# Routing kernel: where the sums of W1's quarters are made, and how the first token group is multiplied

## The chip, the cores and the metric

The kernel runs on one core of a Trainium2 chip. The core has a matrix engine (PE, with its weight loads PEld), a vector engine (DVE), an activation engine (ACT), a general engine (POOL) and a queue engine for transfers (SP), and DMA queues. The metric is the device time of one execution in microseconds. One profiled execution gives a trace, in which times count from the first instruction.

## The reference: attention, routing, experts

The input is q, k, v of 8 batches x 8 heads x 576 positions x 64. First comes a causal attention with a window of 128 and a distance bias per head. Its result is laid out as x, 4608 tokens x 512. Then

```
logits = x @ w_gate ; P = exp(logits - max)            # 4608 x 8
eight times: rows of P to sum 1, columns of P to sum N/E
out = sum over e of P[:, e] * ( relu(x @ w1[e]) @ w2[e] )    # w1: 512 x 1024, w2: 1024 x 512
```

so every token goes through all eight experts, and the expert outputs are weighted by P. As P is not negative, scaling x by P[:, e] ahead of the first layer gives the same result as scaling the output; the kernel uses that for experts 2 to 7.

## The kernel before: stages, queues and order

The schedule is written by hand: every engine takes its instructions in the order in which the program issues them.

**Up to P.** The attention runs block by block. Into it a `Filler` weaves experts 0 and 1, which are multiplied with unscaled x and whose outputs are stored in DRAM (`ysp`) until P is known. The filler deals out pieces: a first-layer piece `l1` (four matmuls of 512 columns, counted as 0.87 us, followed by a ReLU on ACT, L127) or a second-layer piece `l2` (eight matmuls, 1.74 us, followed by a cast on DVE, L555, and later a store on SP, L541). `filler.fill(us)` issues pieces until the given time less 0.3 is reached. Then eight rounds of normalisation of P run on DVE (L825 to L852), with pieces woven in.

**Experts 2 to 7.** From line 861 on, the 36 blocks of 128 tokens are taken as 18 groups of two blocks. A unit is one group with one expert, so there are 18 x 6 = 108 units. A unit computes the first layer of its own expert and, woven in, the second-layer products of the unit before (`product(n - 1, ...)`). The second layer always takes seven products of quarter matrices (a Strassen scheme): the sums of W2's quarters are made once per expert by `sums_of`, five DVE operations of 128x1024 each (L630), and those of the activations by `make_sums` in each unit (L991 to L993).

The first layer has two forms:
- **plain** (`l1_bank`, L953): 32 matmuls of 256 columns in four PSUM banks, each followed by a ReLU on ACT;
- **in seven products** (`part`, L974): 56 matmuls of 128 columns. It needs the sums of W1's quarters from `quads_w1` (four DVE operations of 128x1024, L934; the last one overwrites quarter a21, so the plain form can't be used for that expert behind it), and the sums of x's quarters T1 to T4 from `sums_x` (three DVE operations, L910 to L912). Three PSUM banks A, B and C are filled and copied into each other: A is copied to B (L1126), C to `s5` (L1130), B to C (L1135). L1141 on DVE adds bank B and `s5`, and only then part a22 may go into bank B; L1145 does the same for bank C.

Before the change the first group (units 0 to 5) takes the plain form and all others the other one. `quads_w1` for an expert is called in the unit behind that expert's plain unit.

**Transfers of x.** `scale_x(n)` on ACT multiplies a unit's x with P, two operations (L888); `turn_xs(n)` on SP transposes it with two DMAs (L898). In a unit n both are done for unit n + 2. SP also carries the stores of expert 0 and 1, the loads of their outputs (`load_y`) and the output itself (`finish`).

**Gathering.** A group's seven products add up in the PSUM banks `Ms` over its six experts. The first unit of the next group finishes the last expert's products; `gather` on DVE then adds the banks into `acc` (L1055): products 3, 4, 5 and 2 in that unit, 6, 7 and 1 in the one behind it (`done`). `finish` sends `acc` out.

**The list of sums.** `todo` holds DVE operations that are issued a few at a time by `some(n)`: W2's sums of experts 2 to 4 behind the last attention steps and in the rounds of P, seven more at L857, the rest in units 0 to 4:

```
some((4, 1, 0, 3, 2)[n] if n < 5 else 0)
if 0 < n <= E - 2:
    quads_w1(units[n - 1][1])
```

Of the kernel before, what the change touches and what calls it, by code (L numbers as in the profile page):

```python
# [14 lines left out]
def kernel(  # L15
# [213 lines left out]
    if True:  # L229
# [387 lines left out]
        def extras(e):  # L617
            for n in range(3 if e == E - 3 else e - 1):
                if n not in more:
                    at = dict(tag="a8", bufs=8) if n < 2 else {}  # L620
                    t = (per if n < 2 else lp).tile([P, 4, NF2, HB], FP16, name=f"more_{n}", **at)
                    more[n] = [t[:, i] for i in range(4)]
            return more[e - 2][0:3] if e < E - 3 else [more[n][3] for n in range(3)]

        def sums_of(e, f1, f3, f4):
            q = W2L[e]
            q.update(f1=f1, f3=f3, f4=f4, f6=q["q12"], f7=q["q21"])

            def one(to, x, y, op):
                nc.vector.tensor_tensor(out=q[to], in0=q[x], in1=q[y], op=op)  # L630

            return [
                lambda a=a: one(*a)
                for a in (
                    ("f1", "q11", "q22", ALU.add),
                    ("f3", "q12", "q22", ALU.subtract),
                    ("f4", "q11", "q21", ALU.subtract),
                    ("f6", "q11", "q12", ALU.add),
                    ("f7", "q21", "q22", ALU.add),
                )  # L640
            ]

        def some(n):
            for _ in range(min(n, len(todo))):
                todo.pop(0)()
# [207 lines left out]
        store()  # L853
        filler.fill(1.6)

        todo += sums_of(5, *extras(5))
        some(7)  # L857

# [12 lines left out]
        xs = [xset[i // 2][:, 4 + 2 * (i % 2) : 6 + 2 * (i % 2), :].rearrange("p q n -> p (q n)") for i in range(4)]  # L873

        def strassen(n):
            return n >= E - 2

        def load_x(g):
            for m in range(2):
# [14 lines left out]
        def turn_xs(n):  # L894
            if n >= N:
                return
            for m in range(2):
                nc.sync.dma_start(  # L898
                    out=xset[n % 2][:, 2 * m : 2 * m + 2, :].rearrange("p q (d t) -> p (q d) t", t=P),
                    in_=xs[2 * (n % 2) + m],  # L900
                    transpose=True,
                )
# [11 lines left out]
        def quads_w1(e):  # L914
            w = W1L[e]
            q = dict(a11=w[:, 0:2, 0:HF], a12=w[:, 2:4, 0:HF], a21=w[:, 0:2, HF:Fd], a22=w[:, 2:4, HF:Fd])
            if e < E - 2:
                t = lp.tile([P, 3, 2, HF], FP16, name=f"s_{e}")
                q.update(s1=t[:, 0], s2=t[:, 1], s3=t[:, 2])
            elif e == E - 1:  # L920
                t = per.tile([P, 2, 2, HF], FP16, name=f"s_{e}", tag="xT", bufs=4)
                q.update(s1=t[:, 0], s2=t[:, 1])
                q["s3"] = [per.tile([P, HF], FP16, name=f"s3_{k}", tag="yo", bufs=YO) for k in range(2)]
            else:
                q.update((f"s{i}", aux[:, i].rearrange("p f n -> p (f n)").rearrange("p (k f) -> p k f", k=2)) for i in (1, 2, 3))
            q["s4"] = q["a21"]
            SL[e] = q

            def one(to, a, b, op):
                if isinstance(q[to], list):  # L930
                    for k in range(2):
                        nc.vector.tensor_tensor(out=q[to][k], in0=q[a][:, k], in1=q[b][:, k], op=op)
                else:
                    nc.vector.tensor_tensor(out=q[to], in0=q[a], in1=q[b], op=op)  # L934

            one("s1", "a21", "a22", ALU.add)
            one("s3", "a11", "a21", ALU.subtract)
            one("s2", "s1", "a11", ALU.subtract)
            one("s4", "a12", "s2", ALU.subtract)

        def new_h(n):
            h[n] = per.tile([P, 8, NF2, P], FP16, name=f"hs_{n}", tag="hT", bufs=2)
# [93 lines left out]
        def gather(g, *which):  # L1036
            q4 = acc.rearrange("p m (c n) -> p (m c) n", c=2)
            for m in which:
                bk, half = BANK[m]
                ps = Ms[bk][:, half, :]  # L1040
                for lo, step, op in {
                    1: ((0, 3, ALU.add),),
                    2: ((2, 0, ALU.add), (3, 0, ALU.subtract)),
                    3: ((1, 2, ALU.add),),
                    4: ((0, 2, ALU.subtract),),
                    5: ((0, 0, ALU.subtract), (1, 0, ALU.add)),
                    6: ((3, 0, ALU.add),),
                    7: ((0, 0, ALU.subtract),),
                }[m]:
                    if step:  # L1050
                        a = q4[:, lo : lo + step + 1 : step, :]
                        p2 = ps.unsqueeze(1).to_broadcast([P, 2, HB])
                    else:
                        a, p2 = q4[:, lo, :], ps
                    nc.vector.tensor_tensor(out=a, in0=a, in1=p2, op=op)  # L1055
# [32 lines left out]
        scale_x(0)  # L1088
        scale_x(1)
        turn_xs(0)  # L1090
        filler.fill(3.0)
        while filler.fill(5.0):
            pass
        store()
        load_last(E - 1)
        w2f = per.tile([P, 4, NF2, HB], FP16, name="w2f", tag="w1t", bufs=2)
        todo += sums_of(6, F1_6, w2f[:, 2], w2f[:, 3]) + sums_of(7, aux[:, 0], w2f[:, 0], w2f[:, 1])
        s5y = per.tile([P, 2, GT], FP32, name="s5y", tag="xTt", bufs=1)
        s5 = s5y[:, 0].rearrange("p (f t) -> p f t", f=NF2)
        y = s5y[:, 1].bitcast(FP16).rearrange("p (m d) -> p m d", m=2)  # L1100
        turn_xs(1)
        xs[:] = [per.tile([P, HD], FP16, name=f"xs_{i}", tag="yo", bufs=YO) for i in range(2)] * 2
        late: tuple = ()
        for n in range(N):
            g = units[n - 1][0]
            end = ends(n - 1)
            done, late = late, ()
            if n > 0:
                make_sums(n - 1)
            some((4, 1, 0, 3, 2)[n] if n < 5 else 0)  # L1110
            if 0 < n <= E - 2:
                quads_w1(units[n - 1][1])
            if done:
                gather(units[n - 2][0], 6, 7)
                gather(units[n - 2][0], 1)
            if n > 0 and units[n - 1][1] == 6:
                begin(g, 1)
            y_first_half = n > 0 and units[n - 1][1] == (5 if g == groups[0] else 4)
            if y_first_half:
                begin(g, 0)  # L1120
            if strassen(n):
                new_h(n)
                pa = bank(n, "A")
                part(n, pa, "a11", B11, True)
                pb = bank(n, "B")
                nc.scalar.copy(out=pb, in_=pa)  # L1126
                product(n - 1, 3)
                pc = bank(n, "C")
                part(n, pc, "s1", T1, True)
                nc.scalar.copy(out=s5, in_=pc)  # L1130
                product(n - 1, 4)
                if end:
                    gather(g, 3, 4)
                part(n, pb, "s2", T2)
                nc.scalar.copy(out=pc, in_=pb)  # L1135
                part(n, pa, "a12", B21)
                relu(n, 0, pa)
                scale_x(n + 2)
                product(n - 1, 5, 2)
                part(n, pb, "s3", T3)  # L1140
                nc.vector.tensor_tensor(out=h[n][:, 3], in0=pb, in1=s5, op=ALU.add)  # L1141
                relu(n, 3, h[n][:, 3])
                part(n, pc, "s4", B22)
                turn_xs(n + 2)
                nc.vector.tensor_tensor(out=h[n][:, 1], in0=pc, in1=s5, op=ALU.add)  # L1145
                relu(n, 1, h[n][:, 1])
                sums_x(n + 1)
                if end:
                    gather(g, 5, 2)
                product(n - 1, 6, 7)  # L1150
                part(n, pb, "a22", T4)
                relu(n, 2, pb)
                product(n - 1, 1)
            else:
                pairs = ((3, 4), (5, 2), (6, 7), (1,))
                for i in range(4):
                    l1_bank(n, i)
                    if i == 1:
                        scale_x(n + 2)
                    product(n - 1, *pairs[i])  # L1160
                    if end and i in (0, 1):
                        gather(g, *pairs[i])
                turn_xs(n + 2)
                sums_x(n + 1)
            if done:
                finish(units[n - 2][0])
            if n > 0 and units[n - 1][1] == 2:
                load_y(g, 0)
            if y_first_half:
                load_y(g, 1)  # L1170
            if end:
                late = (6, 7, 1)
            if n == N - E + 2:
                load_w2(E - 1)
# [34 lines left out]
```

## Time and profile before

| what | us |
| --- | --- |
| three runs: median (lowest to highest) | 1025.03 (1024.62 to 1025.8) |
| the profiled execution | 1025.63 |
| its span from first to last instruction | 1023.9 |
| PE busy | 1000.3 |
| DVE busy | 749.5 |
| ACT busy | 722.2 |
| last rounds of P end on DVE | 326.3 |
| expert 1's last pieces end on PE, unit 0 begins | 342.6 |
| unit 6 (the first in seven products) begins | 380.5 |
| unit 107, the last, begins | 1010.1 |

The rounds of P take the stretch up to 326 us, then come the last pieces of experts 0 and 1 up to 342.6, then the units; the change touches the time from 326 us on. A line of the timeline gives start and duration in us, engine, line, operation, output and inputs with their shapes, how many equal ones were merged, and in brackets the idle time of the engine before it with the one who ended it. The end of a matmul is modelled and overlaps the next one's start; the starts are what to go by.

### The profile page before, as it was taken

Reading aid. Unit: us, or ns where it says so; the run is one execution under the profiler, and the core shown is the slowest. Engines: PE = TensorE matmul, PEld = TensorE weight load, DVE = VectorE, ACT = ScalarE, POOL = GpSimd, SP = SyncE. Lnnn points to the kernel's source line nnn. Section 1 sums busy time; section 2 is a strip of 40 time slices with the busy share of each in tenths; the row PEclk is TensorE's granted clock in tenths of the full one; section 3 lists DMA queues with packets and bytes.
Section 4 is the critical chain, followed back from the end, with each engine's and each line's share of the span. In section 5 each row is a group of like instructions: output and inputs, shape, how many; then the busy total and the mean of one; then the engine's idle time right before and its main releaser. Section 6 shows DMA issues by size and latency. Waiting matters only on the chain.

```text
span 1023.9 us, 27787 instructions
## 1 busy us (share of the span) xinstructions
PE 1000.3 (98%) x11487; PEld 801.6 (78%) x11487; DVE 749.5 (73%) x1594; ACT 722.2 (71%) x1240; POOL 78.8 (8%) x143
## 2 busy tenths in 40 slices
PE   7999999999999999999999999999999999999998
PEld 5645444444544698999999999999999999999997
DVE  5735665556578588877877877877887887787787
ACT  7646555555433457888888888888888888888885
POOL 1212033306110000000000000000000000000000
PEclk9999999999999999999999999999999999999999
DMA  9996689889999233343334334324334434333461
GB/s 244 219 271 170 143 221 220 191 196 180 221 192 177 69 72 80 71 81 94 74 64 100 76 66 94 73 64 94 77 65 98 81 71 81 86 82 65 98 115 47
DMA packets 264431, 122.46 MB, mean 120 GB/s; under 512 B 201968, under 2 KB 255728, under 8 KB 264304
## 3 DMA queue, kind: packets, MB, share of 16 engines
q1 hardware_dynamic: 249568, 102.68, 44.2%
q0 software_dynamic: 14304, 17.84, 10.5%
q8 instruction: 90, 1.47, 0.6%
q14 instruction: 37, 0.30, 0.1%
q10 hardware_dynamic: 432, 0.16, 0.1%
HBM read 78.30 MB, written 23.59 MB: 100 GB/s over the span
## 4 chain that ended last, share of the span: by engine, by line
PE 74%; DVE 3%; DMA 1%; ACT 1%; issue 0%; DVEq 0%; ACTq 0%; SPq 0%
PE psM L1011 30%; PE psB L974 13%; PE psA L974 9%; PE psC L974 9%; PE psy L137 5%; PE psh L115 5%; PE psh L953 2%; DVE acc L1055 1%; PE psN L468 1%; DMA acc<-xd 0%; DVE hs L1141 0%; PE psS L412 0%; DVE hs L991 0%; DVE hs L992 0%; DMA s5y<-ysp 0%
## 5 line engine op out<-in xcount | busy, mean ns | idle before, releaser
L1011 PEld LDWEIGHTS <-hs 128*128 128x128 f16 x2996 | 271.7, 98 | 22.4
L1011 PE MATMUL psM<-w2l,hs 128*128 128x256 f16 x1440 | 186.6, 273 | 0.0
L974 PEld LDWEIGHTS <-w1l 128*128 128x128 f16 x2720 | 173.2, 98 | 8.9 <-issue 3.0
L127 ACT ACTIVATE hT<-psh 128x512 f16<-128x512 f32 (+1 forms) x144 | 83.3, 586 | 100.9 <-PE psh L115 100.2
L987 ACT ACTIVATE hs<-hs 128x512 f16<-128x512 f16 x204 | 125.0, 630 | 34.3 <-DVE hs L1141 34.1
L1141 DVE TENSOR_TENSOR hs<-psB,s5y 128x512 f16<-128x512 f32 x102 | 70.4, 690 | 103.7 <-ACT xs L888 95.9
L115 PE MATMUL psh<-xT,w1t 128*128 128x512 f16 (+1 forms) x608 | 139.8, 368 | 3.2 <-DVE xT L517 2.4
L974 PEld LDWEIGHTS <-s 128*128 128x128 f16 x2040 | 135.3, 98 | 5.8
L888 ACT ACTIVATE xs<-xtok,L_sb 128x512 f16<-128x512 f16 x204 | 136.0, 720 | 0.6 <-DMA xset<-xs 0.6
L137 PE MATMUL psy<-w2t,hT 128*128 128x512 f16 x576 | 134.3, 379 | 0.0
L1011 PE MATMUL psM<-more,hs 128*128 128x256 f16 x864 | 129.0, 273 | 0.0
L974 PE MATMUL psA<-xset,w1l 128*128 128x128 f16 x1360 | 103.7, 219 | 0.0
L974 PE MATMUL psB<-xset,s 128*128 128x128 f16 x1360 | 103.7, 219 | 0.0
L137 PEld LDWEIGHTS <-hT 128*128 128x128 f16 x576 | 53.5, 98 | 60.9 <-issue 1.5
L555 DVE CAST yo<-psy 128x512 f16<-128x512 f32 x68 | 46.8, 690 | 72.1 <-PE psy L137 57.8
L115 PEld LDWEIGHTS <-w1t 128*128 128x128 f16 x608 | 54.7, 98 | 54.7 <-issue 7.0
L991 DVE TENSOR_TENSOR hs<-hs 128x1024 f16<-128x1024 f16 x107 | 74.0, 691 | 23.5 <-ACT hs L987 16.8
L430 ACT ACTIVATE pt<-psS 128x1024 f16<-128x1024 f32 (+2 forms) x80 | 67.7, 851 | 29.2 <-PE psS L412 22.7
L1135 ACT COPY psC<-psB 128x512 f32<-128x512 f32 x102 | 58.1, 570 | 36.5 <-PE psB L974 36.5
L1130 ACT COPY s5y<-psC 128x512 f32<-128x512 f32 x102 | 59.8, 586 | 25.5 <-PE psC L974 25.5
L443 DVE TENSOR_TENSOR pt<-pt,mask 128x1024 f16<-128x1024 f16 (+2 forms) x80 | 51.8, 647 | 32.8 <-ACT pt L430 32.7
L1055 DVE TENSOR_TENSOR acc<-acc,psM 128x256 f32<-128x256 f32 (+1 forms) x162 | 74.1, 503 | 2.1
(121 smaller groups left out, 1410.1 us busy)
## 6 DMA issues: line engine op xcount, KB each, us to landing
s5y<-ysp SPq DMA_DIRECT2D x36, 256.0 KB, 3.0
ysp<-yo SPq DMA_DIRECT2D x68, 128.0 KB, 3.3
v<-in_v_dram SPq DMA_DIRECT2D x32, 256.0 KB, 4.4
out_dram<-acc SPq DMA_DIRECT2D x31, 256.0 KB, 2.5
q<-in_q_dram SPq DMA_DIRECT2D x5, 1024.0 KB, 7.8
k<-in_k_dram SPq DMA_DIRECT2D x5, 1024.0 KB, 10.1
xtok<-xd SPq DMA_DIRECT2D x34, 128.0 KB, 2.3
w2t<-in_moe_w_dram POOLq DMA_DIRECT2D x4, 1024.0 KB, 10.9
```

What stands on the lines that cost most here:

```text
L115: nc.tensor.matmul(out=ps[:, 0:nt], lhsT=w1ts[e][:, dt, P * ft : P * ft + P], rhs=xT[:, at : at + nb, dt, :], start=(dt == 0), stop=(dt == ...
L127: nc.scalar.activation(out=st["hT"][:, ft, 0:nt], in_=ps[:, 0:nt], func=AF.Relu)
L137: nc.tensor.matmul(out=ps, lhsT=st["hT"][:, ft, P * ms : P * ms + P], rhs=w2ts[e][:, ft, :], start=(ft == 0), stop=(ft == NFT - 1),)
L430: nc.scalar.activation(out=pt[0:nk, :, 0 : nk + nn], in_=ps[0:nk, :, :, 0 : nk + nn].rearrange("p a y n -> p (a y) n"), func=AF.Exp, scale ...
L888: nc.scalar.mul(out=xs[2 * (n % 2) + m], in_=xtok[m], mul=P_sb[:, blk, e : e + 1])
L974: nc.tensor.matmul(out=ps[:, j, :], lhsT=q[k][:, P * j : P * j + P], rhs=xset[n % 2][:, x, P * k : P * k + P], start=(start and j == 0 and ...
L987: nc.scalar.activation(out=h[n][:, slot], in_=src, func=AF.Relu)
L991: nc.vector.tensor_tensor(out=t[:, 4:6], in0=t[:, 0:2], in1=t[:, 2:4], op=ALU.add)
L1011: nc.tensor.matmul(out=Ms[bk][:, half, :], lhsT=h[n][:, LEFT[m], f, :], rhs=W2L[e][RIGHT[m]][:, f, :], start=(e == 2 and f == 0 and half = ...
L1055: nc.vector.tensor_tensor(out=a, in0=a, in1=p2, op=op)
L1130: nc.scalar.copy(out=s5, in_=pc)
L1141: nc.vector.tensor_tensor(out=h[n][:, 3], in0=pb, in1=s5, op=ALU.add)
```

## The change

- `sums_of(5)` and `some(7)` behind the rounds of P go. In their place the sums of W1 for experts 2, 3 and 4, then W2's sums and W1's sums of expert 5 are put on the list, and while the filler has pieces of experts 0 and 1, one sum is issued behind each piece. What is left then is issued at once (`some(len(todo))`), ahead of the last stores.
- `quads_w1` returns its four operations for the list instead of issuing them. Those of experts 6 and 7 are put on the list behind their W2 sums, and a new table says how many sums each unit issues.
- The first group's units of experts 2 to 6 take the seven-product form; only expert 7's unit stays plain. `sums_x(0)` is called ahead of the loop.
- `turn_xs(1)` is issued right behind `turn_xs(0)`, ahead of the stores of the remaining pieces.
- The gather of product 1, in the second unit of a group, moves from the head of the unit to behind L1141 and its ReLU.

```diff
@@ behind the rounds of P
-        todo += sums_of(5, *extras(5))
-        some(7)
@@ strassen(n)
-            return n >= E - 2
+            return n >= E - 2 or units[n][1] < E - 1
@@ quads_w1(e), at its end
-            one("s1", "a21", "a22", ALU.add)
-            one("s3", "a11", "a21", ALU.subtract)
-            one("s2", "s1", "a11", ALU.subtract)
-            one("s4", "a12", "s2", ALU.subtract)
+            return [
+                lambda a=a: one(*a)
+                for a in (
+                    ("s1", "a21", "a22", ALU.add),
+                    ("s3", "a11", "a21", ALU.subtract),
+                    ("s2", "s1", "a11", ALU.subtract),
+                    ("s4", "a12", "s2", ALU.subtract),
+                )
+            ]
@@ ahead of the loop over units
         turn_xs(0)
-        filler.fill(3.0)
-        while filler.fill(5.0):
-            pass
+        turn_xs(1)
+        for e in range(2, 5):
+            todo += quads_w1(e)
+        todo += sums_of(5, *extras(5)) + quads_w1(5)
+        while filler.fill(0.9):
+            some(1)
+        some(len(todo))
         store()
         load_last(E - 1)
         w2f = per.tile([P, 4, NF2, HB], FP16, name="w2f", tag="w1t", bufs=2)
-        todo += sums_of(6, F1_6, w2f[:, 2], w2f[:, 3]) + sums_of(7, aux[:, 0], w2f[:, 0], w2f[:, 1])
+        todo += sums_of(6, F1_6, w2f[:, 2], w2f[:, 3]) + quads_w1(6)
+        todo += sums_of(7, aux[:, 0], w2f[:, 0], w2f[:, 1]) + quads_w1(7)
...
-        turn_xs(1)
+        sums_x(0)
@@ in the loop over units
-            some((4, 1, 0, 3, 2)[n] if n < 5 else 0)
-            if 0 < n <= E - 2:
-                quads_w1(units[n - 1][1])
+            some({0: 5, 1: 2, 2: 2, 3: 2, 4: 2, 5: 1, 7: 1, 8: 1, 9: 1, 10: 1}.get(n, 0))
             if done:
                 gather(units[n - 2][0], 6, 7)
-                gather(units[n - 2][0], 1)
...
                 relu(n, 3, h[n][:, 3])
+                if done:
+                    gather(units[n - 2][0], 1)
                 part(n, pc, "s4", B22)
```

## The prediction

> **What bounds the kernel now.** I read the page first, then the order of work of PE and DVE around the change, then the same in a later group. The page: PE is the bound.
>
> ```profile
> PE 1000.3 (98%) x11487; PEld 801.6 (78%) x11487; DVE 749.5 (73%) x1594; ACT 722.2 (71%) x1240; POOL 78.8 (8%) x143
> ```
>
> The timeline of PE from 325 to 400 us (start, duration, what; in brackets the idle time before it and who ended it) shows the last four second-layer pieces of expert 1 (L137), then group 0.
>
> ```profile
> 335.65 7.07 PE L137 MATMUL psy<-w2t,hT 128*128 128x512 f16 x32
> 342.56 3.66 PE L953 MATMUL psh<-xset,w1l 128*128 128x256 f16 x32
> 347.79 1.03 PE L953 MATMUL psh<-xset,w1l 128*128 128x256 f16 x8 [1.57 <-DMA xset<-xset]
> ...
> 373.98 1.04 PE L953 MATMUL psh<-xset,w1t 128*128 128x256 f16 x8
> ...
> 380.53 0.61 PE L974 MATMUL psA<-xset,w1l 128*128 128x128 f16 x8
> ...
> 387.90 0.61 PE L974 MATMUL psB<-xset,w1l 128*128 128x128 f16 x8 [1.90 <-DVE hs L1141]
> ...
> 388.78 0.61 PE L974 MATMUL psA<-xset,w1l 128*128 128x128 f16 x8
> ...
> 395.40 0.61 PE L974 MATMUL psA<-xset,w1l 128*128 128x128 f16 x8
> ```
>
> Unit 0 begins at 342.56, unit 1 at 347.79, unit 5 at 373.98, units 6, 7, 8 at 380.53, 388.78 and 395.40. A plain unit with its products costs 6.55 us: (373.98 - 347.79)/4. PE loses 1.57 us to the second turned x and 1.90 us to L1141 in unit 6.
>
> The timeline of DVE over the same stretch: who could be late.
>
> ```profile
> 328.39 0.69 DVE L555 CAST yo<-psy 128x512 f16<-128x512 f32 x1 [2.10 <-PE psy L137]
> 329.00 1.28 DVE L630 TENSOR_TENSOR w2l<-w2l 128x1024 f16<-128x1024 f16 x2
> 330.20 1.89 DVE L630 TENSOR_TENSOR more<-w2l 128x1024 f16<-128x1024 f16 x3
> 332.00 1.28 DVE L630 TENSOR_TENSOR w2l<-w2l 128x1024 f16<-128x1024 f16 x2
> 333.21 0.68 DVE L555 CAST yo<-psy 128x512 f16<-128x512 f32 x1
> 337.58 0.69 DVE L555 CAST yo<-psy 128x512 f16<-128x512 f32 x1 [3.69 <-PE psy L137]
> ...
> 342.76 0.69 DVE L555 CAST yo<-psy 128x512 f16<-128x512 f32 x1 [1.03 <-PE psy L137]
> 343.37 0.68 DVE L630 TENSOR_TENSOR f<-w2l 128x1024 f16<-128x1024 f16 x1
> ...
> 350.81 0.68 DVE L934 TENSOR_TENSOR s<-s,w1l 128x1024 f16<-128x1024 f16 x1
> 351.59 0.69 DVE L934 TENSOR_TENSOR w1l<-w1l,s 128x1024 f16<-128x1024 f16 x1
> ```
>
> Two things: DVE works in written order (the seven sums of `some(7)` stand between the casts as in the code; the cast behind them begins at 333.21 although PE's piece was done at 331.64). And a sum costs 0.60 us from start to start (329.00 to 333.21 is seven), the one that reads the sum just made 0.18 more (350.81 to 351.59).
>
> A later group, DVE then PE: unit 13 begins at 426.32, 14 at 432.63, 15 at 438.82.
>
> ```profile
> 429.56 1.54 DVE L1055 TENSOR_TENSOR acc<-acc,psM 128x256 f32<-128x256 f32 x3
> 431.02 0.68 DVE L1141 TENSOR_TENSOR hs<-psB,s5y 128x512 f16<-128x512 f32 x1
> ```
>
> ```profile
> 426.32 0.61 PE L974 MATMUL psA<-xset,w1l 128*128 128x128 f16 x8
> ...
> 432.63 0.61 PE L974 MATMUL psA<-xset,w1l 128*128 128x128 f16 x8
> ...
> 438.82 0.61 PE L974 MATMUL psA<-xset,w1l 128*128 128x128 f16 x8
> ```
>
> A seven-product unit takes 6.18 us, but the second unit of a group 6.31: three gathers ahead of L1141 push it past the moment when PE needs bank B.
>
> **The change part by part.**
>
> *Sums under the last pieces.* At the loop eleven pieces are left (six first-layer, five casts: the trace has six L127 and five L555 behind the scaling of x at 329.98). The list holds 23 sums: 2 left of expert 4, 12 of W1 for experts 2 to 4, 5 of W2 and 4 of W1 for expert 5. One is issued behind each piece, twelve behind them all. Those ahead of the last cast lie in DVE's idle time (3.69 and about 1.03 before each cast) and cost nothing. The last cast stays at 342.76, since PE sets it; the eleventh sum begins at 343.37, and 13 sums, two of which read the one before, take 13 x 0.60 + 2 x 0.18 = 8.2 us: DVE is free at 351.56. There was no such queue before.
>
> *Unit 0 in seven products.* `sums_x(0)` stands behind that queue. Its first operation took 0.42 (L910), and a waiting PE starts 0.06 behind DVE's end (387.84 to 387.90), so T1 is there at 352.04. PE does part a11 at 342.56 to 343.01 and waits 9.0 us; there are no products of an earlier unit to put in. Then s1, s2, a12, s3, s4 run to about 354.7. `some(5)` stands ahead of L1141: the three x sums end at 352.55 (0.45 + 0.33 + 0.21), five W2 sums at 355.56, L1141 lasts 0.69, and part a22 into bank B starts at 356.30 and takes 0.45. Unit 1 begins at 356.75 against 347.79: +8.96, which contains the 1.57 us saved.
>
> *PE's pace behind that wait.* No wait of 9 us is in the trace; the nearest rows are the first matmuls of the run, on a PE that had done nothing yet, and the next ones of their shape.
>
> ```profile
> 1.05 4.08 PE L249 MATMUL psJ<-ones 128*128 128x256 f16 x20 [1.05 <-DVE ones L651]
> ...
> 5.77 0.60 PE L249 MATMUL psJ<-ones 128*128 128x256 f16 x4
> ```
>
> Twenty in 4.08 us is about 0.2 each, four in 0.60 (less the 0.27 of the last) is 0.11; the slow spell lasts some 3.6 us. Behind idle stretches up to 1.90 us the pace stays full. If PE falls back, s3 ends at 355.45 and L1141 waits for it: +0.14 us, the rest hides under `some(5)`. Ends: 0 (full pace) and +1.5 (slow for two such spells, to about 359.2: 2.8 us past 356.4 at half pace lose 1.4 more). I take +0.14, nearest to the row.
> The Trainium skill ("TensorE: Matmul & The Clock Gate", Part 1) says that PE falls to half clock after an idle window of about 3.4 us and returns after a busy one; windows run free, so by that rule this term would be an estimated 0.1 to 1.4 us and the sum +2.9 to +4.2, where the row alone gives +2.94. No run here has shown the fall behind a wait.
>
> *Units 1 to 4 in seven products.* 4 x (6.55 - 6.18) = 1.48 saved. Their new DVE work hides: make_sums ends some 2.5 us into a unit, two sums end at 3.7 to 3.9, and L1141 is due at 4.25 (436.88 - 432.63). In unit 4 `begin` adds 0.8 us, 0.05 late; in unit 1 ACT's copies of unit 0's end cost 0.03. I take 1.44 saved, 0 to 1.5 possible. Unit 5 stays plain, 6.55; the load of y, 0.5 us late for DVE now, comes earlier since unit 4 frees its x sooner.
>
> *W1 of expert 7 later.* The five DVE operations of 3 us ahead of unit 6's gathers go: unit 6 falls from 8.25 to 6.18, 2.06 saved. In unit 7 (6.62) one sum remains (0.60) and the last gather moves: L1141 is just in time, but `product(n-1, 1)` must wait some 0.2 us until the moved gather has read its bank. 6.40: 0.22 saved, ends 0 and 0.44. Units 8 to 10 take one more sum each in slack of over 1 us.
>
> *x turned ahead of the stores.* SP issues two transposes (2.52 us) before six stores instead of behind them; the stores end with the last cast all the same. POOL's queue is unchanged: its loads of expert 7 were issued at 307 and 318. Cost 0; the gain is counted above. If a store came late, the buffers that it frees are next written by unit 0's scaling, at about 354.
>
> *Gather of product 1 behind L1141.* In unit 13 L1141 could start at 430.57 (unit start + 4.25) once the two other gathers (0.33 each) end near 430.2. The 0.13 us goes: 15 groups x 0.13 + 0.44 in the last (a wait of that size ended at 990.62) = 2.44 saved. L1145 moves from 431.62 to 431.77, its ReLU with it, and the next copy into bank B ends at 434.1, where PE needs it at 434.27; the moved gather ends at 431.85, and bank M1 is due at 432.06. Both fit, with 0.1 to 0.2 us to spare. Ends: 0 and 2.6.
>
> **Sum:** +8.96 + 0.14 - 1.44 - 2.06 - 0.22 - 2.44 = +2.94. The profiled execution took 1025.63 us (span 1023.9 and 1.7 around it), 0.6 above the median of 1025.03. So 1028.6 by that execution, 1028.0 against the median. What a measurement of this kernel can tell from no change is 0.2%, 2.05 us, so the forecast is slower, narrowly.
>
> **Rivals.**
> 1. *The gather's gain doesn't come*, because the later L1145 or the bank of M1 holds PE up as much. For it: slacks of 0.1 to 0.2 us; against: they are positive. +5.4: 1030.4. Chance 0.13.
> 2. *PE stays slow longer*, for two spells of 3.6 us instead of one: 1.4 on top of the forecast, 1029.4. For it: the opening spell; against: one spell lies under `some(5)` almost whole, and the trace shows no second. Chance 0.12. (This is the Trainium skill's rule above at its late end.)
> 3. *A wash:* the last sums come sooner or the gains sum higher, within 2.05 us of before. It takes 1 us in my favourable terms, or two sums fewer at the end. About 1026.3. Chance 0.18.
> 4. *Faster:* the sums fit into DVE's idle time between the casts (five us of it), so that no queue stands behind the last cast. Place: 343.37. Price: 8.2 us of the sum, giving 1025.0 + 2.9 - 8.2 = 1019.8. The point where it decides: each sum less behind the cast is 0.60 us, so with 8 instead of 13 the change breaks even. Against it: one sum per piece, eleven pieces, and written order as seen. Chance 0.07.
>
> **Numbers.** The forecast has 0.50, its own range 1027.0 to 1029.2. Of the forecast and rivals 1 and 2 (0.75) about 0.04 falls inside the bound: slower 0.71; same 0.18 + 0.04 = 0.22; faster 0.07. From 1025.0 to 1031.4 leaves out rival 4, part of the wash and the sum of both slow rivals: under 0.2.
>
> **What would show it.** Right: DVE without idle from the last cast to L1141 of unit 0, some 13.5 us; a PE wait of about 9 us in bank C's part, then one of 1.5 on L1141; units 1 to 4 at 6.18; no wait in unit 6; second units of groups at 6.18. Wrong: T1 ready before 348, fewer than 12 sums behind the last cast, second units still at 6.3 or their successors longer, or matmuls of 128 columns at 0.11 us spacing past 357.

## The result and the profile after

The changed kernel took 1030.61 us (median of six, 1027.89 to 1032.39) against 1024.82 us for the kernel before in the same session (median of six, 1023.56 to 1026.72): ratio 1.0051, 95% interval 1.0033 to 1.0069 (the ratios here and below are the recorded estimates with their intervals; they aren't the quotients of the medians beside them). So it is slower, as forecast; the size forecast was +2.9 us, measured were +5.8. The profiled execution took 1030.17 us, with a span of 1028.2.

The timeline of PE in the changed kernel, around the first group (start, duration, what; in brackets the idle time before it and who ended it):

```profile
337.18 7.07 PE L137 MATMUL psy<-w2t,hT 128*128 128x512 f16 x32
344.08 0.61 PE L977 MATMUL psA<-xset,w1l 128*128 128x128 f16 x8
353.43 1.01 PE L977 MATMUL psC<-xset,s 128*128 128x128 f16 x8 [8.74 <-DVE xset L908]
354.24 1.06 PE L977 MATMUL psB<-xset,s 128*128 128x128 f16 x8
355.09 1.06 PE L977 MATMUL psA<-xset,w1l 128*128 128x128 f16 x8
356.00 1.01 PE L977 MATMUL psB<-xset,s 128*128 128x128 f16 x8
356.81 0.72 PE L977 MATMUL psC<-xset,w1l 128*128 128x128 f16 x8
357.87 0.61 PE L977 MATMUL psB<-xset,w1l 128*128 128x128 f16 x8 [0.34 <-DVE hs L1146]
358.31 0.61 PE L977 MATMUL psA<-xset,w1l 128*128 128x128 f16 x8
...
364.51 0.61 PE L977 MATMUL psA<-xset,w1l 128*128 128x128 f16 x8
...
383.06 1.04 PE L956 MATMUL psh<-xset,w1t 128*128 128x256 f16 x8
...
389.61 0.61 PE L977 MATMUL psA<-xset,w1l 128*128 128x128 f16 x8
...
395.80 0.61 PE L977 MATMUL psA<-xset,w1l 128*128 128x128 f16 x8
...
402.19 0.61 PE L977 MATMUL psA<-xset,w1l 128*128 128x128 f16 x8
```

Unit 0 starts at 344.08, does part a11 and then waits 8.74 us for T1 (L908 is the first operation of `sums_x`). Unit 1 starts at 358.31, unit 5 at 383.06, units 6, 7 and 8 at 389.61, 395.80 and 402.19. Parts s1 to s3 stand 0.8 to 0.9 us apart instead of 0.45: PE runs at half pace behind the wait. The view by windows shows the same in the granted clock (the first column behind the stretch is its length, the number ahead of the DMA share is the clock):

```profile
342.60:352.00 9.40, 2.10 (x16) 1.15 (x15) 8.93 (x15) 0.57 (x1) 0.00 (x0) 0.72 0.10 34
352.00:360.00 8.00, 6.23 (x72) 6.02 (x72) 7.55 (x16) 4.97 (x10) 0.00 (x0) 0.69 0.10 19
```

The timeline of DVE, changed kernel, from the last cast on:

```profile
344.29 0.69 DVE L555 CAST yo<-psy 128x512 f16<-128x512 f32 x1 [0.44 <-PE psy L137]
344.89 1.28 DVE L932 TENSOR_TENSOR s<-w1l 128x1024 f16<-128x1024 f16 x2
346.10 0.68 DVE L932 TENSOR_TENSOR s<-s,w1l 128x1024 f16<-128x1024 f16 x1
346.81 0.69 DVE L932 TENSOR_TENSOR w1l<-w1l,s 128x1024 f16<-128x1024 f16 x1
347.42 1.89 DVE L630 TENSOR_TENSOR more<-w2l 128x1024 f16<-128x1024 f16 x3
349.23 1.28 DVE L630 TENSOR_TENSOR w2l<-w2l 128x1024 f16<-128x1024 f16 x2
350.43 1.28 DVE L932 TENSOR_TENSOR s<-w1l 128x1024 f16<-128x1024 f16 x2
351.64 0.68 DVE L932 TENSOR_TENSOR s<-s,w1l 128x1024 f16<-128x1024 f16 x1
352.35 0.69 DVE L932 TENSOR_TENSOR w1l<-w1l,s 128x1024 f16<-128x1024 f16 x1
352.96 0.42 DVE L908 TENSOR_TENSOR xset<-xset 128x512 f16<-128x512 f16 x1
...
357.12 0.69 DVE L1146 TENSOR_TENSOR hs<-psB,s5y 128x512 f16<-128x512 f32 x1
```

Thirteen sums stand behind the last cast, from 344.89 to 352.96, without a gap; then the x sums, then five more W2 sums ahead of L1146 (L1141 of before).

From these starts, before and after:

| stretch | before | after | difference |
| --- | --- | --- | --- |
| start of the trace to unit 0 | 342.56 | 344.08 | +1.5 |
| unit 0 | 5.23 | 14.23 | +9.0 |
| units 1 to 4 | 26.19 | 24.75 | -1.4 |
| unit 5 | 6.55 | 6.55 | 0 |
| unit 6 | 8.25 | 6.19 | -2.1 |
| unit 7 | 6.62 | 6.39 | -0.2 |
| unit 8 to the end | 628.5 | 626.0 | -2.5 |

From unit 0 on the change costs 2.8 us. The other 1.5 us of the two spans lie ahead of unit 0, where the kernels issue the same instructions up to the last pieces; this stretch differs from trace to trace, which the experiments show.

### The profile page after: what moved, and what is told of

Same layout as the page of the kernel before. It is cut to its first block, busy times and chain, and to the rows that moved or that the text cites. A ratio compares the mean times of both kernels' runs of the same rounds, so it can differ in the third digit from the quotient of the medians.

```text
span 1028.2 us, 28060 instructions
## 1 busy us (share of the span) xinstructions
PE 1000.8 (97%) x11607; PEld 804.3 (78%) x11607; DVE 759.6 (74%) x1619; ACT 730.3 (71%) x1255; POOL 78.8 (8%) x143
## 4 chain that ended last, share of the span: by engine, by line
PE 79%; DVE 3%; ACT 0%; issue 0%; DVEq 0%
PE psM L1014 31%; PE psB L977 14%; PE psA L977 9%; PE psC L977 9%; PE psy L137 7%; PE psh L115 7%; PE psN L468 1%; PE psS L412 1%; DVE s L932 0%; DVE acc L1058 0%; PE psh L956 0%; DVE hs L1146 0%; DVE w2l L630 0%; PE psG L527 0%; DVE more L630 0%; PE psy L1077 0%
## 5 line engine op out<-in xcount | busy, mean ns | idle before, releaser
L977 PEld LDWEIGHTS <-w1l 128*128 128x128 f16 x2880 | 183.9, 98 | 4.7 <-issue 0.5
L990 ACT ACTIVATE hs<-hs 128x512 f16<-128x512 f16 x214 | 131.7, 630 | 33.9 <-DVE hs L1146 24.4
L977 PEld LDWEIGHTS <-s 128*128 128x128 f16 x2136 | 142.7, 98 | 14.9 <-issue 8.9
L1146 DVE TENSOR_TENSOR hs<-psB,s5y 128x512 f16<-128x512 f32 x107 | 74.0, 692 | 103.2 <-ACT xs L886 99.8
L115 PE MATMUL psh<-xT,w1t 128*128 128x512 f16 (+1 forms) x608 | 142.2, 373 | 4.1 <-DVE xT L517 3.7
L977 PE MATMUL psA<-xset,w1l 128*128 128x128 f16 x1440 | 110.2, 220 | 0.0
L977 PE MATMUL psB<-xset,s 128*128 128x128 f16 x1424 | 109.4, 220 | 0.0
L1140 ACT COPY psC<-psB 128x512 f32<-128x512 f32 x107 | 61.0, 570 | 37.4 <-PE psB L977 37.1
L1135 ACT COPY s5y<-psC 128x512 f32<-128x512 f32 x107 | 62.8, 587 | 31.9 <-PE psC L977 31.9
L1131 ACT COPY psB<-psA 128x512 f32<-128x512 f32 x107 | 61.3, 573 | 24.0 <-PE psA L977 24.0
```

Of the source, the lines that this page charges most:

```text
L115: nc.tensor.matmul(out=ps[:, 0:nt], lhsT=w1ts[e][:, dt, P * ft : P * ft + P], rhs=xT[:, at : at + nb, dt, :], start=(dt == 0), stop=(dt == ...
L977: nc.tensor.matmul(out=ps[:, j, :], lhsT=q[k][:, P * j : P * j + P], rhs=xset[n % 2][:, x, P * k : P * k + P], start=(start and j == 0 and ...
L990: nc.scalar.activation(out=h[n][:, slot], in_=src, func=AF.Relu)
```

## The experiments

**The changed kernel again, beside the others.** No edit.

> The changed kernel once more, beside the others. The sum of the prediction says +2.9 us against the kernel before (ratio 1.0029); the units of the first trace add up to +2.8 from unit 0 on, and the rest of the +5.8 between the medians lies ahead of unit 0, in instructions that are the same in both. Theory 'chance': unit 0 starts anywhere between 341 and 346 us and the ratio comes out between 1.002 and 1.005. Rival 'lasting': the stretch ahead of unit 0 is slower with the change every time, unit 0 starts at 344 again and the ratio is 1.005 to 1.006.

Measured: 1028.80 against 1026.60 us (median of 35 runs of the kernel before, 1021.56 to 1031.84), ratio 1.0028 (1.0011 to 1.0046). Unit 0 started at 342.00, and from there to the end the trace shows 684.4 us, against 684.1 in the first trace of this kernel and 681.3 before the change. 'Chance' holds, as far as one more session can tell: the ratio times 1026.60 is +2.9 us, the sum of the prediction, within an interval of +1.1 to +4.7. Over the eight traces of this study unit 0 starts at 341.4 to 345.6 us.

Where the first two traces part, one thing that makes this spread can be seen. The timeline of PE, kernel before, in the attention stage,

```profile
106.33 0.61 PE L412 MATMUL psS<-qN,kN 64*128 64x256 f16 x8
108.30 1.02 PE L115 MATMUL psh<-xT,w1t 128*128 128x512 f16 x4 [1.36 <-DVE xT L517]
109.25 0.56 PE L468 MATMUL psN<-v,pt 128*64 128x65 f16 x8
109.74 2.76 PE L115 MATMUL psh<-xT,w1t 128*128 128x512 f16 x12
```

and the same instructions in the changed kernel:

```profile
105.45 0.61 PE L412 MATMUL psS<-qN,kN 64*128 64x256 f16 x8
108.73 1.87 PE L115 MATMUL psh<-xT,w1t 128*128 128x512 f16 x4 [2.67 <-DVE xT L517]
110.52 0.79 PE L468 MATMUL psN<-v,pt 128*64 128x65 f16 x8
111.24 4.45 PE L115 MATMUL psh<-xT,w1t 128*128 128x512 f16 x12
```

In the changed kernel's timeline of DVE the cast just ahead of this copy is the late one:

```profile
106.92 0.69 DVE L555 CAST yo<-psy 128x512 f16<-128x512 f32 x1 [1.28 <-DMA ysp<-yo]
```

It waited 1.28 us for a store to free its buffer. A PE wait of 1.36 us leaves the pace as it is here; one of 2.67 is followed by some six microseconds at half pace (12 matmuls take 4.45 instead of 2.76 us; the granted clock is 0.79 from 105 to 110 us, 0.53 from 110 to 115 and 1.00 behind). That one place costs 4 us of the early stretch, of which some comes back later: 1.3 us of longer wait, the rest from the slower pace. So a store that came 1.3 us late cost 4 us here.

The granted clock of the other traces fits. In this one the two stretches of 5 us make 2 x 5 x (0.21 + 0.47) = 6.8 us of halved clock. Reckoned so, the clock was halved ahead of unit 0 for about 6.8 us in three traces (the first of the changed kernel, the one with PE kept busy and the one with the x turned late), and these start unit 0 latest, at 344.1 to 345.6; in the other five it was halved for about 3.4 us or, in the kernel before, not at all, and they start it at 341.4 to 343.2. The 35 runs of the kernel before say the same: the eight with a mean granted clock of 1.000 took 1021.56 to 1024.13 us, the twelve with 0.997 or less 1026.80 to 1031.84.

**The move of one gather alone**, in the kernel before:

```diff
-                gather(units[n - 2][0], 1)
...
                 relu(n, 3, h[n][:, 3])
+                if done:
+                    gather(units[n - 2][0], 1)
                 part(n, pc, "s4", B22)
```

> The kernel before with the gather of product 1 moved and nothing else. Theory: the second unit of every group falls from 6.31 to 6.18 us, in the last group but one from 6.62 to 6.18; 2.4 us less than before, ratio 0.9977, and unit 7 loses up to 0.4 more. Rival 1 of the prediction: the later L1145 and the bank of product 1 give it back, ratio 1.000.

Measured: 1023.77 us, ratio 0.9975 (0.9957 to 0.9993); from unit 0 to the end 678.7 against 681.3 us. The timelines of DVE and PE in this kernel, in unit 13, the second unit of the third group:

```profile
428.12 0.75 DVE L1055 TENSOR_TENSOR acc<-acc,psM 128x256 f32<-128x256 f32 x2
429.13 0.69 DVE L1140 TENSOR_TENSOR hs<-psB,s5y 128x512 f16<-128x512 f32 x1 [0.26 <-ACT xs L888]
429.74 0.68 DVE L1055 TENSOR_TENSOR acc<-acc,psM 128x512 f32<-128x512 f32 x1
430.33 0.68 DVE L1146 TENSOR_TENSOR hs<-psC,s5y 128x512 f16<-128x512 f32 x1
```

```profile
424.88 0.61 PE L974 MATMUL psA<-xset,w1l 128*128 128x128 f16 x8
...
431.06 0.61 PE L974 MATMUL psA<-xset,w1l 128*128 128x128 f16 x8
```

DVE now waits 0.26 us ahead of L1140 (L1141 of the kernel before) instead of coming late, and the unit takes 6.18 us instead of 6.31. The unit behind it takes 6.18 too, so neither of the two narrow slacks is eaten up. Rival 1 falls. Unit by unit the 2.6 us are 2.2 from unit 8 on and 0.44 in unit 7, the most that was expected there, less 0.06 in unit 6. In the last group but one the second unit fell from 6.62 only to 6.39, not to 6.18; in the changed kernel it takes 6.18.

**Two sums behind each piece**, in the changed kernel:

```diff
         while filler.fill(0.9):
-            some(1)
+            some(2)
```

> The changed kernel with two sums behind each piece instead of one, so that 22 of the 23 are issued ahead of the last cast or right behind it. Theory (the queue of 13 sums behind the last cast is what unit 0 waits for): the casts move back by about 1.2 us, three sums stay behind the last one, T1 is there some 5 us sooner, PE's wait in bank C's part falls from 8.7 to about 4 us, and the time is 5 us below the changed kernel, 2 below the kernel before. Rival (unit 0 waits for something else, or the later casts hold PE up for lack of free PSUM banks): within 1.5 us of the changed kernel.

Measured: 1023.39 us, ratio 0.9987 (0.9970 to 1.0005); from unit 0 to the end 680.2 us, 3.8 to 4.1 below the changed kernel's two traces. The waits of PE in this kernel, from 335 to 420 us (us in total, how many, the longest):

```profile
PE psC L977 <- DVE xset L908: 4.6, 1, 4.6
```

The wait for T1 fell from 8.7 to 4.6 us and the time with it, so the queue of sums is what unit 0 waits for. The gain was 1 us short of the 5 expected: the casts were pushed back by 2.0 us instead of 1.2, which put T1 0.8 us later, and behind 4.6 us of waiting PE still starts at half pace (granted clock 0.66 from 342 to 352 us), to which I put the rest.

**PE kept busy in the wait**, in the changed kernel:

```diff
+                if n == 0:
+                    spin(aps.tile([P, GT], FP32, name="psJ_u0", tag="pmm", bufs=4), 80)
                 pc = bank(n, "C")
                 part(n, pc, "s1", T1, True)
```

> The changed kernel with 80 matmuls of 128x256 on constants into a spare PSUM bank between part a11 and part s1 of unit 0: about 8.7 us of work in the wait of 9, so that PE is never idle for long there. Theory: the slow spell is hidden under the five W2 sums, all but 0.14 us; the time is that of the changed kernel within 0.5 us, while the matmuls of s1 to s3 are spaced 0.056 us instead of 0.11. Rival 2 of the prediction: the slow spell costs 1.4 us or more, and this kernel is faster by that.

Measured: 1029.72 us, ratio 1.0042 (1.0022 to 1.0062), no faster than the changed kernel beside it (1.0028, 1.0011 to 1.0046). The timeline of PE in this kernel:

```profile
345.64 0.61 PE L977 MATMUL psA<-xset,w1l 128*128 128x128 f16 x8
346.08 8.90 PE L249 MATMUL psJ_u<-ones 128*128 128x256 f16 x80
354.99 0.61 PE L977 MATMUL psC<-xset,s 128*128 128x128 f16 x8
355.43 0.61 PE L977 MATMUL psB<-xset,s 128*128 128x128 f16 x8
...
359.32 0.61 PE L977 MATMUL psB<-xset,w1l 128*128 128x128 f16 x8 [1.40 <-DVE hs L1148]
359.77 0.61 PE L977 MATMUL psA<-xset,w1l 128*128 128x128 f16 x8
```

At full pace s1 takes 0.44 us, and the time won is spent waiting 1.40 us for L1148 (L1146 of the changed kernel). Unit 0 takes 14.13 us, against 14.23 and 14.53 in the two traces at half pace: the slow spell costs 0.1 to 0.4 us, not 1.4. Rival 2 falls at this place. From unit 0 to the end this trace shows 686.0 us, not within 0.5 of the changed kernel's 684.1 and 684.4: 2.0 us more went in unit 104, where a turned x came late. Whether that belongs to the edit isn't shown; no other trace has it.

**The second turned x behind the stores again**, in the changed kernel:

```diff
         turn_xs(0)
-        turn_xs(1)
...
         sums_x(0)
+        turn_xs(1)
```

> The changed kernel with the second unit's x turned behind the stores again, as before the change. Theory: the move is worth nothing here, since unit 1 needs that x only some 14 us behind the start of unit 0; from unit 0 to the end 684.1 to 684.4 us as in the two traces of the changed kernel. Rival: the move is worth the 1.6 us that PE waited for this x before the change, and the stretch takes 685.7 or more.

Measured: 1030.37 us against 1024.85 (median of 23 runs of the kernel before), ratio 1.0032 (1.0010 to 1.0054); from unit 0 to the end 684.3 us. The move of the transposes is worth nothing in this kernel: unit 0's own wait covers them.

**The same work, spread out**, in the changed kernel:

```diff
-        todo += sums_of(5, *extras(5)) + quads_w1(5)
-        while filler.fill(0.9):
-            some(1)
-        some(len(todo))
+        todo += sums_of(5, *extras(5))
+        for i in range(11):
+            filler.fill(0.9)
+            some((2, 2, 2, 2, 1, 1, 1, 1, 2, 2, 0)[i])
+            if i == 6:
+                sums_x(0)
+        assert not filler.fill(0.9)
+        todo += quads_w1(5)
...
-        sums_x(0)
...
-            some({0: 5, 1: 2, 2: 2, 3: 2, 4: 2, 5: 1, 7: 1, 8: 1, 9: 1, 10: 1}.get(n, 0))
+            some({0: 4, 1: 1, 2: 2, 3: 2, 4: 1, 5: 3, 7: 1, 8: 1, 9: 1, 10: 1}.get(n, 0))
...
+            some({0: 1, 1: 2, 2: 2, 3: 1, 4: 2}.get(n, 0))
             if done:
                 finish(units[n - 2][0])
```

> The changed kernel with the same work in another order: sixteen sums behind the eleven pieces (two behind most of the early ones), the x sums of unit 0 ahead of the last four casts, and the rest dealt out over units 0 to 5, four at the head of unit 0 and one to three elsewhere, part of them at a unit's end. Nothing is left out. Theory: no queue stands between the last cast and unit 0, PE's waits of 8.7 us (T1) and on the first L1146 go, unit 0 takes about 4.5 us instead of 14.2, units 1 to 4 6.2 each, and from unit 0 to the end the trace shows about 674.5 us against 681.3 before the change; ratio to the kernel before 0.9935. Rival (DVE hasn't room for these sums in units 0 to 4, which is what the kernel before avoided): waits on DVE come back in those units and the ratio is 0.997 or above.

Measured: 1020.21 us against 1024.85, ratio 0.9941 (0.9922 to 0.9960): faster than the kernel before by some 6 us and than the changed kernel by more. From unit 0 to the end 674.9 us. The timeline of PE in this kernel:

```profile
343.15 0.61 PE L977 MATMUL psA<-xset,w1l 128*128 128x128 f16 x8
343.60 0.61 PE L977 MATMUL psC<-xset,s 128*128 128x128 f16 x8
...
347.79 0.61 PE L977 MATMUL psB<-xset,w1l 128*128 128x128 f16 x8 [0.96 <-DVE hs L1149]
348.23 0.61 PE L977 MATMUL psA<-xset,w1l 128*128 128x128 f16 x8
...
354.43 0.61 PE L977 MATMUL psA<-xset,w1l 128*128 128x128 f16 x8
```

Unit 0 takes 5.08 us instead of 14.23: T1 is ready when PE comes to it, and 0.96 us on DVE, with two waits of 0.26 us on ACT, is what remains (I had expected 4.5 us in all). Units 1 to 4 follow at 6.2 us each and the plain unit 5 at 6.55 (unit 6 starts at 379.53 in this trace). So DVE has room for the sums, if they are put into its gaps. Sixteen of them stand ahead of the last cast, the other seven went into units 0 to 5. The time is close to the 1019.8 us that rival 4 of the prediction gave for a change without the queue.

## Why the prediction was right

- *DVE's queue:* 8.2 us of sums behind the last cast were forecast; they took 8.07 (344.89 to 352.96). Thirteen stood there, as counted, and DVE went on without a wait to the end of L1146, 13.5 us behind the last cast, as forecast.
- *Unit 0:* +8.96 and 0.14 for the pace, so 14.33 us; measured 14.23, 14.53 and 14.43 in the three traces that keep this order (the third is the one with the x turned late), and 14.13 with PE kept busy.
- *PE's pace:* it fell behind the wait of 8.74 us. Matmuls of 128 columns stand about 0.106 us apart there (32 in 3.38 us, from 353.43 to 356.81) instead of 0.055 (8 in 0.44 us with PE kept busy), for 3.6 us in the first trace (353.43 to about 357.0) and about 5 in three others. The spell's price on the path is 0.1 to 0.4 us, because the five W2 sums ahead of L1146 last almost as long. So of the 1.5 us that PE was to wait for L1141 only 0.34 is seen as a wait in the first trace; with PE kept busy, and so at full pace, it was 1.40. That the pace fell is as the Trainium skill's rule ("TensorE: Matmul & The Clock Gate", Part 1) has it, and the traces agree with the rule that the spell's length varies. They differ from it on the wait that is enough: the rule asks for an idle window of about 3.4 us, and in the attention stage a wait of 2.67 us was enough. At this one place the lower end of the range that the rule gave, 0.1 to 1.4 us, was the right one.
- *Units 1 to 4:* 1.44 saved, forecast 1.44. *Unit 6:* 2.06, forecast 2.06. *Unit 7:* 0.23, forecast 0.22.
- *The gather:* 2.5 us from unit 8 on in the first trace, 2.2 alone in the kernel before (2.6 with units 6 and 7); forecast 2.44. By the terms written down, 15 x 0.13 + 0.44, it would have been 2.39 and the sum +2.99.
- *The sum:* +2.94 forecast; +2.8 and +3.05 from unit 0 on in the two traces of the changed kernel (684.08 and 684.35 against 681.30), and 1.0028 in the larger comparison.
- *The total was off.* The first measurement, 1030.61 us, lies above the forecast's own range (1027.0 to 1029.2) and right beside the 1030.4 of rival 1. By that number alone rival 1 would have been taken for true; it is the units at 6.18 and the gather moved alone that rule it out. The direction and the terms from unit 0 on were right for the reasons given; that the first total still fell between 1025.0 and 1031.4 owes something to luck.
- *What the prediction had no term for:* the first measurement's +5.8. A part of it, 1.5 us in the profiled pair, lies ahead of unit 0 in unchanged instructions. I took the spread of that stretch to be as small as that of the three runs shown (1.2 us); 35 runs of the kernel before spread over 10 us. What of the rest of the difference is chance, and whether the change makes late transfers in the attention stage likelier, was not tried, and the cause of the first session's larger difference stays open. The six later comparisons give no sign of such an effect: their ratios come to +2.9, -2.6, -1.3, +4.3, +3.3 and -6.0 us, in the order above, and the traces from unit 0 to the end to +3.1, -2.6, -1.1, +4.6, +3.0 and -6.4 against the kernel before. For the same reason my bound of 0.2% for what a measurement can tell was too tight: the intervals here are about 0.2% to either side, with ten or twelve runs against 23 or 35.

## What to carry to other kernels

Work that is taken off a later stage must go where its engine is idle, not just earlier: count the instructions that will stand in the queue between the last one that the old stage needs and the first that the new stage needs, and price that queue, because it is all on the path. One sum per piece put eight microseconds of sums in front of the next stage, while DVE still idled some four ahead of the last five casts. Two per piece where the gaps are long, the next stage's own first operations ahead of the last casts, and the rest dealt out over the units turned a loss of 0.3% into a gain of 0.6%; two per piece alone took the loss away and no more (0.9987, 0.9970 to 1.0005). A wait that an engine just misses by a tenth of a microsecond, repeated in every group, is worth as much as one stall of two microseconds: the gather's move alone gained 0.25%, most of it so.

## What the runs showed of the hardware that was not expected

- A wait of 2.67 us on PE in the attention stage was enough for half pace (granted clock 0.53 from 110 to 115 us), while 1.36 and 1.90 us in the kernel before were not. The length of one wait doesn't decide alone. In the second trace of the changed kernel a wait of 1.87 us, up to 146.43, was followed by half clock (0.50 from 149 to 151 us), and in the first one of 1.88 us, up to 149.34, was not (1.00 from 149 to 155). In the kernel with two sums per piece, 4.6 us ahead of unit 0 were enough too.
- Half pace costs little where another engine is late anyway (0.1 to 0.4 us in unit 0) and more where PE has its work at hand (in the attention stage 16 matmuls of 512 columns took some 2.5 us longer: 1.87 + 4.45 against 1.02 + 2.76).
- Identical instructions ahead of unit 0 ended between 341.4 and 345.6 us in eight traces, so a single profiled pair can't be read off its spans alone; the stretch from unit 0 to the end repeated to 0.3 us in the two traces of the changed kernel.
